# Gated linear attention and a gated MLP on one core: first batch in pairs of chunks

## The chip, the cores and the metric

The kernel runs on one core of a Trainium2 chip. A core has TensorE (PE in the profile; PEld is its loading of weights), VectorE (DVE), ScalarE (ACT), GpSimd (POOL) and SyncE (SP), and 16 DMA engines between the main memory and the on-chip memory of 128 partitions. TensorE writes to PSUM, which has eight banks of 128 partitions by 512 floats; DVE and ACT read it from there. The metric is the device time of one execution, in microseconds (us).

## The reference

Two layers, one after the other. The first is a recurrence over 768 tokens for 4 batches and 8 heads, with a 48 by 48 state:

```python
for t in range(S):
    state = alpha[:, :, t, :, None] * state + np.einsum('bhd,bhe->bhde', k[:, :, t], v[:, :, t])
    y[:, :, t] = np.einsum('bhd,bhde->bhe', q[:, :, t], state)
```

Its output, with the heads side by side, is x (4 x 768 x 384). The second layer mixes it:

```python
h = np.maximum(x @ w_in, 0.0)                      # 384 -> 1024
u, v = h[..., :512], h[..., 512:]
v_n = (v - mean(v)) / np.sqrt(var(v) + 1e-06)      # over the 512
v_s = np.einsum('ts,bsd->btd', w_spatial, v_n) + b_spatial[None, :, None]
out = (u * v_s) @ w_out                            # 512 -> 384
```

All arrays are float32 in main memory; the kernel multiplies in bf16.

## The kernel before

**First layer** (`first(i)`, i = 6 b + c). A batch is cut into six chunks of 128 tokens, one token per partition. For each chunk SP loads alpha, k, q and v (`ac`, `kc`, `qc`, `vc`, 192 KB each, rows of 48 floats; L231). ACT takes the logarithm of alpha (`la`, L268). A matmul with a triangle of ones gives its running sum over the tokens, and four one-column matmuls give its total per pair of heads (`cum`, L289 and L299). ACT makes `binv` = exp(−sum), `bc` = exp(total) and exp(sum); POOL multiplies k by `binv` (`kt`, L322), DVE multiplies q by exp(sum) (`qt`, L358), POOL casts v (`vb`, L366). TensorE transposes `kt` and `qt` in four 128x128 blocks each, in two PSUM banks (L375), and DVE or ACT copies each out (`kT`, `qT`). Scores are eight matmuls of 48 rows by 128 columns, two heads side by side in two row halves of the array (`pt`, L465); DVE multiplies them by a triangular mask (`ptm`, L477); `y` is eight matmuls of 48 columns with the masked scores (L494), and four of 96 columns with the state of the chunks before (L488). The state's growth is four matmuls of 96 columns over 128 output rows (`tp`, L421), of which the two diagonal halves are used: DVE adds them to the old state in two instructions on 64 partitions each (L438), POOL multiplies by `bc` (L447) and casts to `sbd` (L454, L455). y is cast, transposed in three blocks (L513) and copied to `xT`.

**Second layer**, per batch: `second_v` (v, relu, mean and variance, `vn`), `second_u`, `second_s` (the spatial mix: six matmuls of 384 columns per group, eight groups; bias added by DVE from `bsp_bc`, product with u on POOL, L664) and `second_o` (four matmuls per 128 tokens, a copy, a store on SP, L684). They share helper lines: L559 is every matmul of the second layer, L136 and L138 are copies on ACT and DVE. In the last batch the bias is put in by a matmul of one row (`ones_row` by `b_sp_sb`) at the head of each of the eight groups, and one DVE multiply ends a group (L648). `w_spatial` is transposed on TensorE once (`weights`, L570).

**Order.** Nothing is left to a scheduler at run time: each step is an `Op` with an engine, an estimated duration, dependencies, a priority and the PSUM slots that it takes. `schedule()` (L50) places the operations by estimated start and priority, and emits them in that order; every engine then runs its own list in order and waits by semaphores. PSUM has rings of two banks for `a` (cum, tp, y), two for `p` (transposes, scores) and four for `p2` (second layer). Loads and stores share SP's queue; w_in, w_spatial, w_out and the bias (a broadcast to 128 partitions, L702, and a row, L703) are loaded by POOL. Loads have four buffers (alpha, q) or six (k, v); stores have four. A path for two chunks at once is in the code, switched off by `FOLD = 0`.

## Time and profile before

| | |
|---|---|
| median of 3 runs | 169.93 us (169.17 to 170.67) |
| profiled execution | 169.51 us, of it 167.7 us span |
| busy: PE, PEld | 138.7 us, 87.1 us |
| busy: DVE, ACT, POOL | 123.0, 104.8, 85.5 us |
| DMA | 26.61 MB, mean 159 GB/s, 95% of the packets under 512 B |
| mean granted TensorE clock | 0.990 |

Times in the profile are microseconds from the span's start. "Busy" is the time in which an engine had an instruction under way; matmuls overlap, so a busy PE is not PE at its peak. A group is named by line, engine, operation, output and inputs, with the number of its instructions, their busy time, the mean of one in ns, and the idle time of the engine just before them with what ended it. In the slices, a digit is the busy share of a fortieth of the span in tenths.

### The profile page before, as it was taken

How to read it: one execution, taken by the hardware profiler on the slowest of the kernel's cores; microseconds unless marked ns; L12 is line 12 of the kernel's file. 1: busy time of each engine (PE TensorE's matmuls, PEld its weight loads, DVE VectorE, ACT ScalarE, POOL GpSimd, SP SyncE). 2: the span in 40 equal slices, each digit the busy share in tenths (PEclk: the TensorE clock that was granted, in tenths of full speed). 3: DMA queues.
4: the chain of work that ended last, by engine and by line, in shares of the span. 5: the costliest groups of instructions: out<-in, count | busy, mean ns of one | idle time of the engine just before them, and what ended most of it. 6: DMA issues, size and time to landing. Idle time of an engine off the chain costs nothing.

```text
span 167.7 us, 3952 instructions
## 1 busy us (share of the span) xinstructions
PE 138.7 (83%) x1402; PEld 87.1 (52%) x1412; DVE 123.0 (73%) x278; ACT 104.8 (62%) x255; POOL 85.5 (51%) x155
## 2 busy tenths in 40 slices
PE   0364687984579998999959999998999999999991
PEld 0252446553446765664526576664666665544450
DVE  7564568996648899879899787679999970883410
ACT  3432445984458846778869647998997546970042
POOL 7742508583152899953264898844369972000000
PEclk9999999999959999999999999999999999999999
DMA  5999989999699897396999891899992005200025
GB/s 115 217 181 209 223 164 215 170 201 253 133 197 219 167 218 145 86 287 154 215 217 210 172 216 51 209 266 181 199 227 56 0 4 207 76 0 4 0 101 182
DMA packets 105140, 26.61 MB, mean 159 GB/s; under 512 B 100320, under 2 KB 104672, under 8 KB 105120
## 3 DMA queue, kind: packets, MB, share of 16 engines
q1 hardware_dynamic: 103296, 23.60, 65.9%
q0 software_dynamic: 1824, 2.75, 9.1%
q8 instruction: 11, 0.18, 0.5%
q14 instruction: 9, 0.07, 0.1%
HBM read 23.99 MB, written 4.72 MB: 171 GB/s over the span
## 4 chain that ended last, share of the span: by engine, by line
PE 55%; DMA 13%; DVE 10%; ACT 9%; POOL 6%; issue 4%; DVEq 0%; POOLq 0%; ACTq 0%
PE ps L559 36%; DMA ac<-in_alpha_dram 6%; PE pt L375 5%; DMA w_in_sb<-in_moe_w_in_dram 5%; PE pt L465 3%; POOL kt L322 3%; PE y L513 3%; PE cum L289 2%; DMA qc<-in_q_dram 2%; PE tp L421 2%; DVE ptm L477 2%; ACT uT L142 2%; PE y L488 2%; DVE vn L612 2%; PE y L494 2%
## 5 line engine op out<-in xcount | busy, mean ns | idle before, releaser
L559 PE MATMUL ps<-w_spT,vn 128*128 128x384 bf16 x192 | 38.3, 326 | 0.0
L322 POOL TENSOR_TENSOR kt<-kc,binv 128x384 bf16<-128x384 f32 x24 | 21.9, 912 | 27.2 <-ACT bc L317 19.1
L477 DVE TENSOR_TENSOR ptm<-pt,mask 128x512 bf16<-128x512 f32 x48 | 31.1, 683 | 4.2 <-PE pt L465 3.9
L664 POOL TENSOR_TENSOR gT<-vsb,uT 128x384 bf16<-128x384 f32 x24 | 21.6, 912 | 2.3 <-DVE vsb L652 2.2
L559 PEld LDWEIGHTS <-vn 128*128 128x128 bf16 x192 | 16.4, 97 | 9.4 <-issue 1.4
L136 ACT COPY o_sb<-ps 128x384 f32<-128x384 f32 x22 | 10.5, 482 | 16.6 <-PE ps L559 16.1
L559 PE MATMUL ps<-w_in_sb,xT 128*128 128x512 bf16 x62 | 18.1, 407 | 2.7 <-DMA w_in_sb<-in_moe_w_in_dram 1.8
L594 DVE BATCH_NORM_STATS2 stats<-v_sb 128x6 f32<-128x512 bf16 x24 | 16.3, 678 | 5.3 <-ACT v_sb L142 5.3
L559 PE MATMUL ps<-xT,w_in_sb 128*128 128x384 bf16 x96 | 18.9, 328 | 0.7 <-ACT v_sb L142 0.7
L142 ACT ACTIVATE v_sb<-ps 128x512 bf16<-128x512 f32 x24 | 14.2, 595 | 6.0 <-PE ps L559 5.9
L559 PE MATMUL ps<-w_out_sb,gT 128*128 128x384 bf16 x96 | 17.7, 326 | 0.0
L310 ACT ACTIVATE binv<-cum 128x384 bf16<-128x384 f32 x24 | 11.8, 490 | 8.8 <-PE cum L299 6.6
L268 ACT ACTIVATE la<-ac 128x384 bf16<-128x384 f32 x24 | 12.5, 522 | 7.1 <-DMA ac<-in_alpha_dram 4.6
L366 POOL CAST vb<-vc 128x384 bf16<-128x384 f32 x24 | 12.1, 506 | 9.3 <-DMA vc<-in_v_dram 8.6
L358 DVE TENSOR_TENSOR qt<-qc,cum 128x384 bf16<-128x384 f32 x24 | 13.2, 550 | 4.5 <-DMA qc<-in_q_dram 2.1
L447 POOL TENSOR_TENSOR state<-state,bc 128x192 f32<-128x192 f32 x20 | 10.2, 512 | 11.2 <-DVE state L438 4.5
L652 DVE TENSOR_TENSOR vsb<-ps,bsp_bc 128x384 f32<-128x384 f32 x24 | 13.2, 554 | 2.9 <-PE ps L559 2.4
L289 PE MATMUL cum<-la,ut_ones 128*128 128x384 bf16 x24 | 8.8, 368 | 7.8 <-ACT la L268 7.8
L136 ACT CAST x_sb<-y 128x384 bf16<-128x384 f32 x24 | 11.5, 485 | 4.9 <-PE y L494 4.6
L375 PE MATMUL pt<-ident,kt 128*128 128x128 bf16 x96 | 10.2, 234 | 4.8 <-POOL kt L322 4.2
L142 ACT ACTIVATE uT<-ps 128x384 bf16<-128x384 f32 x30 | 13.6, 497 | 0.7 <-PE ps L559 0.7
L438 DVE TENSOR_TENSOR state<-tp,state 64x192 f32<-64x192 f32 x32 | 11.2, 350 | 3.7 <-PE tp L421 3.4
(75 smaller groups left out, 253.4 us busy)
## 6 DMA issues: line engine op xcount, KB each, us to landing
ac<-in_alpha_dram SPq DMA_DIRECT2D x24, 192.0 KB, 3.7
kc<-in_k_dram SPq DMA_DIRECT2D x24, 192.0 KB, 3.8
qc<-in_q_dram SPq DMA_DIRECT2D x24, 192.0 KB, 3.7
vc<-in_v_dram SPq DMA_DIRECT2D x24, 192.0 KB, 3.8
out_dram<-o_sb SPq DMA_DIRECT2D x24, 192.0 KB, 2.0
wsp_nat<-in_moe_w_spatial_dram POOLq DMA_DIRECT2D x1, 1152.0 KB, 13.1
w_in_sb<-in_moe_w_in_dram POOLq DMA_DIRECT2D x1, 768.0 KB, 8.6
w_out_sb<-in_moe_w_out_dram POOLq DMA_DIRECT2D x1, 384.0 KB, 7.7
```

The costliest lines, as they stand in the source:

```text
L136: nc.scalar.copy(out=out, in_=in_)
L142: nc.scalar.activation(out=out, in_=in_, func=AF.Relu)
L268: nc.scalar.activation(out=la[:, :, :, 0:D], in_=quad(st["ac"]), func=AF.Ln)
L289: nc.tensor.matmul(out=cm[:, 0:DM], lhsT=ut_ones, rhs=la[:, :, :, 0:D], start=True, stop=True)
L322: nc.gpsimd.tensor_mul(out=kt[:, :, :, 0:D], in0=quad(st["kc"]), in1=st["binv"])
L358: nc.vector.tensor_mul(out=qt[:, :, :, 0:D], in0=quad(st["qc"]), in1=st["cv"])
L375: nc.tensor.transpose(hold["t"][:, hp, :], src[:, hp, :, :], ident)
L477: nc.vector.tensor_tensor(out=st["ptm"][:, s], in0=st[f"pt{s}"], in1=mask4, op=ALU.mult)
L559: return lambda ps: nc.tensor.matmul(out=out(ps), lhsT=lhsT(), rhs=rhs(), start=start, stop=stop)
L594: nc.vector.bn_stats(out=stats, in_=d["v_sb"][:, tt, :])
L652: nc.vector.tensor_tensor(out=hold["vs"], in0=ps[:, 0:TH], in1=bsp_bc[:, th, :], op=ALU.add)
L664: nc.gpsimd.tensor_tensor(out=bt[b]["gT"][:, dsl, cols], in0=hold["vs"], in1=bt[b]["uT"][:, dsl, cols], op=ALU.mult)
```

## The change

Batch 0 is computed in three pairs of chunks (`pair(j)`). Each of its 12 loads (`load_pair`) brings 256 tokens, two neighbouring tokens to a partition, in rows of 96 floats. Chunk 0 of a pair then lies in partitions 0 to 63 and chunk 1 in 64 to 127, and each step is done for the even and the odd tokens (`par`): the running sums are two accumulating matmuls for each parity, the state's growth, the scores and the scores' part of y work on 64-row halves, and scores and growth also on 64-column halves of the array. The pair's sums and transposes use the `p2` banks.

In batches 1 to 3, q and k are transposed together into one bank and copied out by one instruction of 1024 columns, and the state's growth is eight matmuls of 48 columns on 64-column halves, so that DVE adds the state in one instruction on 128 partitions (in batch 0 as well).

`schedule()` now counts TensorE's activity in windows and doubles durations outside warm ones; where an operation that takes PSUM slots would leave TensorE idle before 24 us of its own reckoning, it puts matmuls of a constant tile (`junk`, up to 192 columns each) ahead of that operation, into the same bank. It also treats DMA as an engine with a duration for each transfer.

The bias is no longer broadcast by DMA: two one-row matmuls and two copies make `bsp_bc` (`bias()`); in the last batch only the last of the eight groups keeps its one-row matmul, and the others add and multiply as in the other batches, the product on POOL or DVE. Constants are set in three lots, two of them later; load buffers are six chunks for all four inputs, store buffers six. w_in is issued after the first logarithm, w_spatial and the bias after that of the third pair, w_out after its last q product.

The core of the diff (a line of "..." marks what is left out):

```diff
+class Clock:
+
+
+    TICK, ENOUGH = 3.4133, 3100.0
+
+    def __init__(self):
+        self.count = {}
+
+    def warm(self, t):
+        return self.count.get(int(t / self.TICK) - 1, 0.0) >= self.ENOUGH
+
+    def run(self, t, dur, cols):
+
+        end = t + dur * (1.0 if self.warm(t) else 2.0)
+        x = t
+        while x < end - 1e-9:
+            k = int(x / self.TICK + 1e-9)
+            y = min(end, (k + 1) * self.TICK)
+            self.count[k] = self.count.get(k, 0.0) + cols * (y - x) / (end - t)
+            x = y
+        return end
...
+        if eng == "PE":
+            if op.take and start < warm_to:
+                t = max([free.get(eng, 0.0), warm_from] + [slot.ring.free_at(k) for k, slot in enumerate(op.take)])
+                while True:
+                    each = 0.00042 if clock.warm(t) else 0.00084
+                    cols = min(192, int((start - t) / each) // 32 * 32)
+                    if cols < 96:
+                        break
+                    fill.append(cols)
+                    t = clock.run(t, 0.00042 * cols, cols)
+            end = clock.run(start, dur, op.cols)
...
+    def bank(pool, shape, dtype, **kw):
+
+        t = pool.tile(shape, dtype, **kw)
+        flat = t if len(shape) == 2 else t.rearrange("p a b -> p (a b)")
+        for cols in fill:
+            nc.tensor.matmul(out=flat[:, 0:cols], lhsT=junk[:, 0:128], rhs=junk[:, 0:cols], start=True, stop=True)
+        fill.clear()
+        return t
...
+        nc.vector.memset(junk, 0.5)
...
+    def dma(key, us, emit, deps, prio, eng="SP", issue=0.4):
+        o = op(key + ("issue",), eng, issue, emit, deps + [xfers[-8] if len(xfers) >= 8 and key[0] in LOADS else None],
+               prio=prio)
+        x = op(key, "DMA", us, lambda _: None, [o], prio=prio, lat=2.0)
+        if key[0] in LOADS:
+            xfers.append(x)
+        return x
...
+        def z(_):
+            st["state"] = work.tile([128, HP, D], FP32, name="state")
+            if c == 0:
+                nc.vector.tensor_copy(out=st["state"], in_=st["tp"])
+            else:
+                nc.vector.tensor_tensor(out=st["state"], in0=st["tp"], in1=T[i - 1]["state"], op=ALU.add)
+
+        op(("z", i), "DVE", 0.27, z, got(("upd", i), ("S", i - 1), ("sb", i - WK)), prio=P + 8, use=[st["sl_t"]])
...
+    def pair(j):
+
+        st = T[2 * j]
+        P = float(20 * j)
+        t0 = 2 * j * C
+        EV = {"DVE": 0.34, "ACT": 0.48}
+
+        def halves(ci):
+            return slice(64 * ci, 64 * ci + 64)
+
+        def ln(_):
+            nc.scalar.activation(
+                out=lap_bufs[j][:, :, :, 0:D], in_=st["ac"].rearrange("p h two d -> p two h d"), func=AF.Ln)
+
+        op(("lnp", j), "ACT", 0.73, ln, got(("acp", j), ("cz", j - 1)), prio=P + 1)
...
+            def cum(_, par=par, last=last):
+                cm = st[f"cum{par}"] = bank(pp_2, [128, 512], FP32, name="ps2")
+                for p2 in range(2):
+                    nc.tensor.matmul(
+                        out=cm[:, 0:DM], lhsT=lt_pair if p2 > par else le_pair, rhs=lap_bufs[j][:, p2, :, 0:D],
+                        start=(p2 == 0), stop=(p2 == 1))
+                if not last:
+                    rows = halves(par)
+                    for hp in range(HP):
+                        for p2 in range(2):
+                            nc.tensor.matmul(
+                                out=cm[:, DM + hp:DM + hp + 1],
+                                lhsT=lap_bufs[j][rows, p2, 2 * hp:2 * hp + 2, :].rearrange("p s d -> p (s d)"),
+                                rhs=ones_col[rows], start=(p2 == 0), stop=(p2 == 1))
+
+            op(("cump", j, par), "PE", 0.33 + 0.2, cum, got(("lnp", j)), prio=P + 2, take=sl_c[par], cols=768)
...
+            for nm, bufs in (("k", ktp_bufs), ("q", qtp_bufs)):
+                hold = {}
+                sl = Slot(rings["p2"])
+
+                def tr(_, par=par, bufs=bufs, hold=hold):
+                    pt = bank(pp_2, [128, 512], FP32, name="ps2")
+                    hold["t"] = pt.bitcast(BF16).rearrange("p (n t) -> p n t", n=8)[:, 0:HP, :]
+                    for hp in range(HP):
+                        nc.tensor.transpose(hold["t"][:, hp, :], bufs[j][:, par, hp, :, :], ident)
+
+                op(("tr", nm, j, par), "PE", 0.25, tr, got((nm + "tp", j, par)), prio=P + 5, take=sl, cols=512)
...
+                for hp in range(HP):
+                    for s in range(2):
+                        for par in range(2):
+                            nc.tensor.matmul(
+                                out=T[i]["tp"][64 * s:64 * s + 64, hp, :], lhsT=ktp_bufs[j][rows, par, hp, s, :],
+                                rhs=st["vb"][rows, par, 2 * hp + s, :], start=(par == 0), stop=(par == 1))
+
+            op(("upd", i), "PE", 0.43, upd,
...
+            def sc(_, par=par):
+                for s in range(2):
+                    st[f"pt{s}{par}"] = bank(pp_p, [128, HP, 128], FP32, name="pt")
+                for hp in range(HP):
+                    for s in range(2):
+                        for ci in range(2):
+                            rows = slice(64 * s, 64 * s + D)
+                            nc.tensor.matmul(
+                                out=st[f"pt{s}{par}"][halves(ci), hp, :], lhsT=st["kT"][rows, par, hp, halves(ci)],
+                                rhs=q_cols(rows, hp, ci), start=True, stop=True)
...
+                rows = halves(ci)
+                n, tot = 0, 2 * H + (HP if i else 0)
+                for h in range(H):
+                    for par in range(2):
+                        nc.tensor.matmul(
+                            out=yt[:, h, :], lhsT=st[f"ptm{par}"][rows, h % 2, h // 2, :],
+                            rhs=st["vb"][rows, par, h, :], start=(n == 0), stop=(n == tot - 1))
+                        n += 1
+                if i:
+                    for hp in range(HP):
+                        nc.tensor.matmul(
+                            out=yt[:, 2 * hp:2 * hp + 2, :].rearrange("p s d -> p (s d)"),
+                            lhsT=q_cols(slice(0, 128), hp, ci), rhs=sbd_bufs[(i - 1) % NB][:, hp, :],
+                            start=False, stop=(n == tot - 1))
...
+        def tr_qk(_):
+            pt = bank(pp_p, [128, 512], FP32, name="pt")
+            t = hold["t"] = pt.bitcast(BF16).rearrange("p (n t) -> p n t", n=8)
+            for n, src in enumerate((kt, qt)):
                 for hp in range(HP):
-                    nc.tensor.transpose(hold["t"][:, hp, :], src[:, hp, :, :], ident)
...
+                    nc.tensor.transpose(t[:, HP * n + hp, :], src[:, hp, :, :], ident)
+
+        def ev_qk(eng):
+            st["kqT"] = work.tile([128, 2, HP, C], BF16, name="kqT", bufs=4).rearrange("p a h c -> p (a h) c")
+            copy(eng, st["kqT"], hold["t"])
...
+        op(("trk", i), "PE", 0.46, tr_qk, got(("kt", i), ("qt", i), ("y", i - WK)), prio=P + 5, take=sl, cols=1024)
...
-                st["tp"] = pp_a.tile([128, HP, 2 * D], FP32, name="tp", tag="a")
+                st["tp"] = bank(pp_a, [128, HP, D], FP32, name="tp", tag="a")
                 for hp in range(HP):
-                    nc.tensor.matmul(
-                        out=st["tp"][:, hp, :], lhsT=kt[:, hp, :, :],
-                        rhs=st["vb"][:, 2 * hp:2 * hp + 2, :].rearrange("p s d -> p (s d)"),
-                        start=True, stop=True)
...
+                    for s in range(2):
+                        nc.tensor.matmul(
+                            out=st["tp"][64 * s:64 * s + 64, hp, :], lhsT=kt[:, hp, s, :],
+                            rhs=st["vb"][:, 2 * hp + s, :], start=True, stop=True)
+
+            st["sl_t"] = Slot(rings["a"])
+            op(("upd", i), "PE", 0.25, upd, got(("kt", i), ("vb", i), ("sb", i - WK), ("S", i - 1)), prio=P + 7, take=st["sl_t"], cols=384)
...
     def second_s(b, dsl, th):
-        tail = b == B - 1
+        last = b == B - 1 and dsl == NDS - 1 and th == 1
         mms = []
-        if tail:
+        if last:
             mms.append(mm(
                 lambda ps: ps[:, 0:TH], lambda: ones_row, lambda: b_sp_sb[:, th * TH:(th + 1) * TH], True, False))
         for st in range(NT):
...
+              us + got(("be", th)) + [made.get(("o", b - 2, x)) for x in range(NT)], parts=2, pdeps=pdeps)
+        if last:
             made[("g", b, dsl, th)] = made[("s", b, dsl, th)]
         else:
-            def gm(_):
-                nc.gpsimd.tensor_tensor(
+            def gm(eng):
+                ENG[eng].tensor_tensor(
                     out=bt[b]["gT"][:, dsl, cols], in0=hold["vs"], in1=bt[b]["uT"][:, dsl, cols], op=ALU.mult)
 
-            op(("g", b, dsl, th), "POOL", 0.82, gm, got(("s", b, dsl, th)), prio=Q)
+            op(("g", b, dsl, th), {"POOL": 0.82} if b < B - 1 else {"POOL": 0.82, "DVE": 0.46}, None, gm, got(("s", b, dsl, th)), prio=Q)
 
...
     def b_sp(_):
-        nc.gpsimd.dma_start(out=bsp_bc, in_=moe_b_spatial[None, :].to_broadcast([128, S]))
         nc.gpsimd.dma_start(out=b_sp_sb, in_=moe_b_spatial[None, :])
 
...
+    def load_pair(j):
+        st = T[2 * j]
+        t0 = 2 * j * C
+        for n, (name, src) in enumerate((("ac", alpha), ("kc", k), ("qc", q), ("vc", v))):
+            def emit(_, name=name, src=src):
+                t = io_pool.tile([128, 2, H, D], FP32, name=name)
+                t = st[name] = t.rearrange("p a h d -> p (a h d)").rearrange("p (h two d) -> p h two d", two=2, d=D)
+                nc.sync.dma_start(
+                    out=t.rearrange("p h two d -> p h (two d)"),
+                    in_=src[0, :, t0:t0 + 2 * C, :].rearrange("h (p two) d -> p h (two d)", two=2))
+
+            dma((name + "p", j), 1.52, emit, [], LOADPRIO[j][n])
...
+        if j == 0:
+            dma(("w_in",), 2.2, w_in, got(WIN), 0.0, "POOL", 1.0).lat = 8.0
+            op(("consts2",), "POOL", 2.5, constants2, got(("sb", 1)), prio=60.0)
+        if j == 2:
+            dma(("w_sp",), 3.3, w_sp, got(WSP), 0.0, "POOL", 1.0).lat = 8.0
+            dma(("b_sp",), 0.1, b_sp, got(WSP), 0.0, "POOL", 1.0)
+            dma(("w_out",), 1.1, w_out, got(WOUT), 0.0, "POOL", 1.0).lat = 8.0
...
-    schedule(ops)
+    schedule(ops, fill, 2.0, WARM)
```

496 lines of the change are left out of this document (265 added, 231 removed).

## The prediction

> **What bounds the kernel now.** I read the page first: the span in slices, then the DMA queues.
>
> ```profile
> PE   0364687984579998999959999998999999999991
> PEclk9999999999959999999999999999999999999999
> DMA  5999989999699897396999891899992005200025
> q1 hardware_dynamic: 103296, 23.60, 65.9%
> q0 software_dynamic: 1824, 2.75, 9.1%
> ```
>
> PE is half idle in the first eleven slices (46 us) while DMA stands at 9; after that PE stands mostly at 9. So there are two stages, and I cut the trace there with the view by stretches of time (columns: length, then busy time and instructions of PE, PEld, DVE, ACT, POOL, then granted clock, DMA share, GB/s).
>
> ```profile
> 0.00:46.20 46.20, 26.57 (x301) 19.10 (x305) 32.55 (x80) 23.39 (x55) 23.11 (x52) 1.00 1.00 189
> 46.20:164.00 117.80, 112.13 (x1101) 68.03 (x1107) 90.41 (x198) 80.92 (x200) 62.39 (x104) 0.99 0.67 147
> 40.00:50.00 10.00, 6.20 (x81) 4.59 (x83) 5.05 (x11) 4.62 (x9) 3.33 (x6) 0.83 0.90 188
> 80.00:90.00 10.00, 7.40 (x69) 4.63 (x71) 9.22 (x21) 7.92 (x24) 3.38 (x7) 1.00 1.09 215
> 164.00:167.70 3.70, 0.00 (x0) 0.00 (x0) 0.00 (x0) 0.48 (x1) 0.00 (x0) 1.00 0.45 163
> ```
>
> Up to 46.2 us the DMA share is 1.00, and PE is busy 26.57 us of 46.2: loads bound this stage. From 46.2 to 164 PE is busy 112.13 of 117.8 us and DMA has room (0.67): PE, with what feeds it, bounds that one. Then the last store lands. The chain of waits (start, length, what) says the same:
>
> ```profile
> 4.51 0.53 ACT la L268
> 7.11 8.62 DMA w_in_sb<-in_moe_w_in_dram
> 36.70 9.45 DMA ac<-in_alpha_dram
> 76.92 3.75 DMA qc<-in_q_dram
> 141.82 22.19 PE ps L559 x120
> 164.08 0.48 ACT o_sb L136
> ```
>
> The first work starts at 4.51, the chain hangs 8.62 us on w_in and 9.45 us on an alpha load that is queued behind the weights, once more on a q load at 77, and ends in matmuls. The execution took 169.51 us for a span of 167.7 (1.8 outside), 0.4 under the median of 169.93; I sum on 169.51 and add 0.4.
>
> **The change part by part.**
>
> *Fewer, longer packets for batch 0: −6.3 us of DMA.*
>
> ```profile
> ac<-in_alpha_dram SPq DMA_DIRECT2D x24, 192.0 KB, 3.7
> out_dram<-o_sb SPq DMA_DIRECT2D x24, 192.0 KB, 2.0
> bsp_bc<-in_moe_b_spatial_dram POOLq DMA_DIRECT2D x1, 384.0 KB, 7.9
> ```
>
> A chunk load is 1024 packets of 192 B (128 tokens by 8 heads by 48 floats); a store is 128 packets of 1536 B. After 164 us only stores move: 163 GB/s x 3.7 us = 603 KB, three stores, in 0.45 x 3.7 = 1.67 us of all 16 engines, so 0.55 us each, 69 ns per packet on one engine (8 packets each). Queue q1 took 0.659 x 167.7 = 110.5 us; less 24 x 0.55 = 13.3 leaves 97.2 us for 96 loads: 1.01 us each, 15.8 ns per packet. A line through the two points gives 0.0396 ns per byte, so 23.4 ns for the new 384 B packet and 64 x 23.4 = 1.50 us for a pair load, against 2.02 for the two loads it replaces. Twelve pair loads save 12 x 0.52 = 6.3 us. No row has a packet of 384 B: if a packet costs by the byte, the saving is 0; if by the count alone, 12.1. I take the line, since its ends are both measured. The Trainium skill, "DMA: Bandwidth & Descriptors" (Specifications), says that transfers under 512 B are done as a read-modify-write; both 192 and 384 lie under it. The measured rise from 11 to 22 B per ns between 192 and 1536 B does not tell where it happens, so the time by that rule is a rival below.
>
> *Bias no longer broadcast by DMA: −2.2 us of DMA.* q0 took 0.091 x 167.7 = 15.3 us for 2.75 MB; bsp_bc is 0.39 MB of it: 2.2 us (1.2 if what is read counts, where the weights are twice as large). It lies in the queue ahead of the alpha load at 36.70. Two matmuls and two copies replace it, in PE's idle part of the first stage.
>
> Together 8.5 us at a share of 1.00: the first stage can end at about 37.7 instead of 46.2. The other moves on the queues: SP issues the same bytes in 12 fewer instructions; w_in on POOL's queue goes out after the first Ln instead of after the first kt, some 1.5 us earlier; w_sp, w_out and the bias row stay behind the last third of batch 0, as before.
>
> *Batch 0 costs PE more.* Prices from start to start in a dense part of the order of time:
>
> ```profile
> 121.80 0.33 PE L289 MATMUL cum<-la,ut_ones 128*128 128x384 bf16 x1
> 121.96 0.24 PE L299 MATMUL cum<-ones_col,la 128*128 128x1 bf16 x4
> 122.07 0.65 PE L559 MATMUL ps<-xT,w_in_sb 128*128 128x384 bf16 x3
> ...
> 127.96 0.33 PE L421 MATMUL tp<-vb,kt 128*128 128x96 bf16 x4
> 128.13 0.65 PE L559 MATMUL ps<-w_spT,vn 128*128 128x384 bf16 x3
> 128.72 0.40 PE L465 MATMUL pt<-qT,kT 48*128 48x128 bf16 x8
> 129.05 0.34 PE L513 MATMUL y<-ident,x_sb 128*128 128x128 bf16 x3
> ...
> 137.68 0.36 PE L494 MATMUL y<-vb,ptm 128*128 128x48 bf16 x8
> 137.88 0.81 PE L559 MATMUL ps<-w_out_sb,gT 128*128 128x384 bf16 x4
> ```
>
> A 384-column matmul takes 0.16 us, four one-column ones 0.11, four of 96 columns 0.17, eight score matmuls 0.33, eight of 48 columns 0.20. Per pair: two more 384-column and eight more one-column matmuls for the sums of logarithms, 0.32 + 0.22 = 0.54; 32 instead of 16 scores, +0.66; state update 32 of 48 columns for 8 of 96, 0.80 − 0.34 = +0.46; 16 more matmuls of 48 columns in y, +0.40. That is 2.1 us, 6.2 for three pairs. Four tiles of 64x64 may run beside each other, so the scores may add nothing: 4.2.
>
> Changing the shape of the array costs on top. Its price stands in the tail, where a one-row bias matmul opens each group:
>
> ```profile
> 149.27 0.33 PE L559 MATMUL ps<-b_sp_sb,ones_row 1*128 1x384 bf16 x1
> 149.53 0.66 PE L559 MATMUL ps<-w_spT,vn 128*128 128x384 bf16 x3
> 150.13 0.33 PE L559 MATMUL ps<-b_sp_sb,ones_row 1*128 1x384 bf16 x1
> ```
>
> From 149.27 to 150.13 are 0.86 us for the bias and three full matmuls; three take 0.48, so the bias costs 0.37, of which 0.16 is its own and 0.21 the way into and out of another shape. A pair makes about eight such round trips (sums, updates, scores, y, twice each) where two chunks made two: +1.3, +3.8 for three. So batch 0 adds 4 to 10 us of PE. PE's cover in the first stage is 46.2 − 26.6 = 19.6 us idle, 11 once the stage is 8.5 shorter, but the 4.5 before the first Ln, and waits inside the first pair, can't be filled. I charge 3 us, between 0 and 10. The longer chain of a pair is a rival.
>
> *Junk matmuls and the clock: −0.8 us.*
>
> ```profile
> 26.41 0.52 PE L494 MATMUL y<-vb,ptm 128*128 128x48 bf16 x8
> 30.76 0.36 PE L494 MATMUL y<-vb,ptm 128*128 128x48 bf16 x8
> 42.42 0.36 PE L494 MATMUL y<-vb,ptm 128*128 128x48 bf16 x8
> ```
>
> The same eight matmuls take 0.52 us at 26.4 and 0.36 at 30.8 and later: PE starts slow though the clock row shows 9, and after the wait at 44 to 46 the clock row falls to 5 (0.83 over 40 to 50 us, 1.7 us of work lost). While loads bound the stage, a faster PE shortens only the steps between a landing and the next, so the early warmth pays little. If the wait for alpha goes, the 1.7 goes; I count half. A junk matmul of 192 columns stands in PE's queue ahead of real work where the planner's times are late: by the row of 384 columns, at half speed, under 0.2 us each, at most one per wait. Between −1.7 and +1.
>
> *64-column state update in batches 1 to 3: +2.3 us.* 15 chunks go from four matmuls of 96 columns (0.17) to eight of 48 (0.20 by the y row, 0.10 if two run side by side), and enter and leave a new shape: 0.21. Bounds 15 x (−0.07) = −1.0 and 15 x 0.24 = 3.6; I take 0.15 a chunk, as some sit next to the scores, which change shape anyway. The Trainium skill, "TensorEngine Tiling (Array Packing)" (Key Properties), says that a change of tiling mode drains TensorE; the bias rows agree, with 0.21 us. By that rule every one of the 15 pays, and the sum would be 1.3 higher.
>
> *Bias in the tail: −2.6 us.* Seven of the eight one-row matmuls go, at 0.37. They lie on the last 22.19 us of the chain. In their place DVE adds and POOL or DVE multiplies; eight groups of some 1 us each leave room for one 0.55 add each, and the last group keeps its matmul, so what is late is no later.
>
> *DVE and SP in the second stage: −1.8 us.*
>
> ```profile
> L438 DVE TENSOR_TENSOR state<-tp,state 64x192 f32<-64x192 f32 x32 | 11.2, 350 | 3.7 <-PE tp L421 3.4
> L477 DVE TENSOR_TENSOR ptm<-pt,mask 128x512 bf16<-128x512 f32 x48 | 31.1, 683 | 4.2 <-PE pt L465 3.9
> L138 DVE COPY qT<-pt 128x512 bf16<-128x512 bf16 x14 | 5.9, 418 | 1.5 <-PE pt L375 1.3
> ```
>
> One state add instead of two saves DVE 0.35 us a chunk, the merged copy some 0.1. PE is the bound there, so I count 0.5 us in all (0 to −3). The merged transposes wait for both q and k; the matmuls of the earlier batch that fill PE stand ahead of or behind them, and the price is inside these bounds. PE idles 2.6 us between 80 and 90, after the q load at 76.92 that left SP's queue late; ac and qc buffers grow from four to six chunks and stores from four to six, so I count half, −1.3 (0 to −2.6).
>
> **Sum.** −8.5 + 3.0 − 0.8 + 2.3 − 2.6 − 0.5 − 1.3 = −8.4: 161.1, and 161.5 against the median.
>
> **Rivals.**
>
> *A. The forecast:* 161.5; its own range by the terms 157 to 166. Chance 0.60.
>
> *B. A packet costs by the byte up to a store's size.* The 6.3 us stay, but then the slower first stage hides all that batch 0 adds (3.0): 161.1 + 6.3 − 3.0 + 0.4 = 164.8; with the wait for alpha left, 165.6. For it: nothing between 192 and 1536 B is measured. Against: the line. The Trainium skill's rule on transfers under 512 B ("DMA: Bandwidth & Descriptors", Specifications) would do this here. Chance 0.13.
>
> *C. The pair's chain becomes the bound, slower.* Chunk 0 took from 4.51 to its last copy:
>
> ```profile
> 13.19 0.48 ACT L136 COPY xT<-y 128x384 bf16<-128x384 bf16 x1 [0.73 <-PE y L513]
> ```
>
> ```profile
> L358 DVE TENSOR_TENSOR qt<-qc,cum 128x384 bf16<-128x384 f32 x24 | 13.2, 550 | 4.5 <-DMA qc<-in_q_dram 2.1 <-ACT cum L353 2.0
> ```
>
> 9.2 us. A pair repeats the DVE steps (one 0.55, two copies of 0.42, two masks of 0.68, 0.70 of state: 3.4) and four ACT steps of 0.5 (as the la and xT rows): 14.6 us. If the three pairs run one after another, y of the last ends at 4.5 + 3 x 14.6 = 48.3 instead of 42.8: +5.5, no gain from DMA, the second stage's terms −2.1: 169.9 + 3.4 = 173.3. The gain is gone from 12.8 us a pair, and over 14.0 the kernel is slower by 1%. Against: y of chunks 2 and 3 stand 4.35 us apart (26.41, 30.76), so chunks do overlap. Chance 0.08.
>
> *D. The second stage also had slack:* PE's busy time counts overlapping matmuls (0.33 us for one that gives way after 0.16). If the lighter DVE and PSUM use let PE close up, and batch 0 hides all its extra: 161.5 − 3.0 − 2.5 (DVE to its bound) − 1.0 = 155. Chance 0.15.
>
> *E. The gain is eaten inside TensorE:* batch 0 shows all its 10 us and every update its bound, 161.5 + 7 + 1.3 = 169.8. Chance 0.04.
>
> **How the numbers follow.** About 1% is what a measurement here can tell from no change. Faster by over 1% (under 168.2): A, B, D nearly whole, 0.86. Slower (over 171.6): C, less the part where the chain is only a little too long, 0.07. Same: 0.07. The range 155 to 168.5 takes A, B and D's upper half, and leaves out C, E and D's far end.
>
> **What would show it.** Right: DMA at 9 from the start with the first stage ending near 38; pair loads near 1.5 us of engine time; no 8.6 us on w_in; the last 120 matmuls some 2.6 us shorter; tp groups with a gap of 0.1 on either side. Wrong: pair loads at 2 us (B); PE or DVE at 9 already in batch 0, with y of chunk 5 after 42 us (C); PE's second stage shorter than its 117.8 us by far more than 4 (D).

## The result and the profile after

Before took 169.55 us in these runs (median of 4, 167.97 to 170.67), after 163.16 us (4 runs, 162.83 to 163.89): a ratio of 0.966, with a 95% interval of 0.958 to 0.974. The profiled execution of after took 163.89 us, 162.1 of it span. Some executions of a kernel come out over 1.5% longer than its fastest: medians are of all executions, ratios leave these out.

The page of after, the span in 40 slices and the DMA queues:

```profile
PE   7599798089999999989999999999999999999991
PEclk9959999557999999999999999999999999999999
DMA  5999999999979898897999998989700002600025
q1 hardware_dynamic: 90816, 23.60, 66.4%
q0 software_dynamic: 1744, 2.36, 8.2%
```

PE is fuller than before in the first eleven slices, but there is a 0 in the eighth slice (28.4 to 32.4 us), and from that slice on the clock row reads 5, 5, 7. The view by stretches, with the same columns as in the prediction, cut where chunk 7's sum of logarithms begins and where the last copy begins:

```profile
0.00:47.35 47.35, 37.30 (x563) 27.13 (x564) 32.30 (x76) 25.34 (x58) 20.07 (x45) 0.86 1.04 208
47.35:158.55 111.20, 109.12 (x1156) 68.84 (x1155) 89.34 (x187) 75.01 (x185) 65.37 (x106) 1.00 0.64 142
27.80:33.20 5.40, 0.01 (x1) 0.01 (x1) 0.01 (x1) 0.95 (x3) 0.64 (x1) 0.56 1.21 206
30.00:40.00 10.00, 6.80 (x70) 4.59 (x71) 4.56 (x11) 4.62 (x10) 0.10 (x1) 0.57 1.09 195
40.00:50.00 10.00, 9.84 (x149) 6.68 (x147) 7.97 (x18) 8.80 (x22) 4.91 (x10) 1.00 0.92 181
80.00:90.00 10.00, 9.63 (x97) 5.86 (x96) 9.83 (x25) 9.53 (x27) 5.46 (x11) 1.00 0.97 198
```

Three marks split both spans. Chunk 7's sum of logarithms (the first `cum` row in each fence) is the first; the first matmul of the tail's spatial mix (149.27 before, 146.28 after) the second; the start of the last copy the third (164.08 before, 158.55 after). In order of time, first before, then after:

```profile
46.75 0.48 PE L289 MATMUL cum<-la,ut_ones 128*128 128x384 bf16 x1 [2.69 <-ACT la L268]
...
54.63 0.33 PE L289 MATMUL cum<-la,ut_ones 128*128 128x384 bf16 x1
```

```profile
47.35 0.32 PE L581 MATMUL cum<-lap,ut_ones 128*128 128x384 bf16 x1
...
52.77 0.33 PE L581 MATMUL cum<-lap,ut_ones 128*128 128x384 bf16 x1
...
146.28 6.99 PE L735 MATMUL ps<-w_spT,vn 128*128 128x384 bf16 x42
153.20 0.33 PE L735 MATMUL ps<-b_sp_sb,ones_row 1*128 1x384 bf16 x1
```

| | before, us | after, us | change | forecast |
|---|---|---|---|---|
| start to chunk 7's sum | 46.75 | 47.35 | +0.6 | −6.3 (−8.5 + 3.0 − 0.8) |
| to the tail's spatial mix | 102.52 | 98.93 | −3.6 | +0.5 (+2.3 − 0.5 − 1.3) |
| to the start of the last copy | 14.81 | 12.27 | −2.5 | −2.6 |
| to the end of the span | 3.62 | 3.55 | −0.1 | 0 |

The total came near the forecast of 161.5, and two of its three parts did not. The first stage, where nearly the whole gain was to come from, gained nothing. The chain of waits of after says what holds it (start, length, what):

```profile
19.62 12.61 DMA vc<-in_v_dram
32.25 0.51 ACT vbp L180
...
158.55 0.48 ACT o_sb L180
```

The wait of 8.62 us for w_in and that of 9.45 us for an alpha load are gone, but one of 12.61 us for v of the third pair stands in their place. The order of time around it, on four engines:

```profile
7.37 1.44 SPq L905 DMA_DIRECT2D qc<-in_q_dram  x1
...
20.29 0.89 POOL L890 DMA_DIRECT2D wsp_nat<-in_moe_w_spatial_dram  x1
...
21.46 0.83 ACT L371 ACTIVATE lap<-ac 128x768 bf16<-128x768 f32 x1
...
32.25 0.51 ACT L180 CAST vbp<-vc 128x384 bf16<-128x384 f32 x1 [6.70 <-DMA vc<-in_v_dram]
...
33.20 0.50 PE L342 MATMUL y<-ident,x_sb 128*128 128x128 bf16 x3 [5.52 <-ACT x_sb L180]
```

SP issues v at 19.62, POOL issues w_spatial (1152 KB) 0.7 us later, and v lands 12.6 us after its issue. Meanwhile ACT stands 6.70 us at the cast of v; copies of y of chunks 2 and 3 (`x_sb`) are queued behind it, so PE, which has nothing else, waits 5.52 us for `x_sb`. From 27.8 to 33.2 PE is busy for 0.01 us. In before w_spatial went out at 27.79:

```profile
27.79 0.90 POOL L696 DMA_DIRECT2D wsp_nat<-in_moe_w_spatial_dram  x1
```

### The profile page after: what moved, and what is told of

It is laid out like the page before. It is cut to its first block, busy times and chain, and to the rows that moved or that the text cites. A ratio compares the mean times of both kernels' runs of the same rounds, so it can differ in the third digit from the quotient of the medians.

```text
span 162.1 us, 4501 instructions
## 1 busy us (share of the span) xinstructions
PE 146.4 (90%) x1718; PEld 96.0 (59%) x1718; DVE 121.6 (75%) x263; ACT 100.8 (62%) x243; POOL 85.4 (53%) x151
## 4 chain that ended last, share of the span: by engine, by line
PE 55%; SPq 11%; DVE 10%; DMA 8%; ACT 8%; POOL 4%; issue 3%; ACTq 0%; DVEq 0%; POOLq 0%
PE ps L735 37%; SPq L905 11%; DMA vc<-in_v_dram 8%; PE pt L633 4%; PE y L342 2%; DVE ptm L674 2%; POOL gT L856 2%; DVE stats L786 2%; PE pt L663 2%; ACT cum L611 2%; PE tp L649 2%; DVE qtp L616 2%; PE cum L581 2%; PE ps L746 1%; ACT x_sb L180 1%
## 5 line engine op out<-in xcount | busy, mean ns | idle before, releaser
L856 POOL TENSOR_TENSOR gT<-vsb,uT 128x384 bf16<-128x384 f32 x28 | 25.5, 922 | 19.9 <-DVE vsb L844 19.7
L674 DVE TENSOR_TENSOR ptm<-pt,mask 128x512 bf16<-128x512 f32 x36 | 23.3, 683 | 2.9 <-PE pt L663 2.7
L735 PE MATMUL ps<-w_in_sb,xT 128*128 128x512 bf16 x72 | 19.6, 396 | 0.2 <-ACT xT L180 0.2
L844 DVE TENSOR_TENSOR vsb<-ps,bsp_bc 128x384 f32<-128x384 f32 x31 | 16.5, 554 | 3.0 <-PE ps L735 2.5
L605 POOL TENSOR_TENSOR ktp<-kc,binv 128x384 bf16<-128x384 f32 x18 | 16.5, 917 | 3.0 <-POOL sbd L321 1.3
L342 PE MATMUL y<-ident,x_sb 128*128 128x128 bf16 x72 | 8.4, 228 | 6.5 <-ACT x_sb L180 6.5
L735 PEld LDWEIGHTS <-gT 128*128 128x128 bf16 x96 | 8.9, 98 | 5.5
L735 PEld LDWEIGHTS <-w_in_sb 128*128 128x128 bf16 x96 | 8.5, 97 | 5.8 <-issue 0.2
L342 PEld LDWEIGHTS <-x_sb 128*128 128x128 bf16 x72 | 5.2, 100 | 9.9 <-ACT x_sb L180 7.8
L182 DVE COPY xT<-y 128x384 bf16<-128x384 bf16 x10 | 4.2, 416 | 8.8 <-PE y L342 8.7
L616 DVE TENSOR_TENSOR qtp<-qc,cum 128x384 bf16<-128x384 f32 x18 | 9.8, 547 | 0.8 <-ACT cum L611 0.8
```

The costliest lines, as they stand in the source:

```text
L342: nc.tensor.transpose(xv[:, ks, :], st["x_sb"][:, ks, :], ident)
L605: nc.gpsimd.tensor_mul(out=kt[:, :, :, 0:D], in0=quad(st["kc"]), in1=st["binv"])
L616: nc.vector.tensor_mul(out=qt[:, :, :, 0:D], in0=quad(st["qc"]), in1=st["cv"])
L674: nc.vector.tensor_tensor(out=st["ptm"][:, s], in0=st[f"pt{s}"], in1=mask4, op=ALU.mult)
L735: return lambda ps: nc.tensor.matmul(out=out(ps), lhsT=lhsT(), rhs=rhs(), start=start, stop=stop)
L844: nc.vector.tensor_tensor(out=hold["vs"], in0=ps[:, 0:TH], in1=bsp_bc[:, th, :], op=ALU.add)
```

## The experiments

The theories were: (1) the early w_spatial load takes the bandwidth from v and with it the first stage's gain; (2) the 64-column update, the junk matmuls or the longer chain of a pair cost what is missing; and for the middle, whether it gained from the update, from the buffers, or from what the first stage hands on. Each ratio is to executions of before made beside that run on the same chip; their medians lie between 167.44 and 168.24 us.

### w_spatial later

The loads of w_spatial and of the bias row are issued right before that of w_out; the written order of everything else stays.

```diff
@@ w_sp, b_sp (issue after the third pair's logarithm)
-        nc.gpsimd.dma_start(out=..., in_=...)
+        pass
@@ w_out
+        w_sp_late()
+        b_sp_late()
```

> The changed kernel with one move: the loads of w_spatial and of the bias row are issued right before that of w_out (about 27 us) instead of at 20 us; the order of everything else is kept. Theory 1 (the weights' long packets hold back v of the third pair, which landed 12.6 us after its issue, and all engines stand from 27.8 to 33.2): v lands within 6 us of its issue, the stand of 5.4 us goes, PE's clock stays up, and the kernel takes 158 to 160 instead of 163.2; what may be late next is w_spatial itself at its transposes, up to 2 us. Theory 2 (batch 0 is bound by TensorE or by the pair's chain, not by that load): 162.2 to 163.5.

Measured: 159.6 us (159.32 to 163.31, 4 runs), ratio 0.959 (0.946 to 0.972). The profiled execution has a span of 157.6. Its DMA issues (KB each, median us to landing), after's row first and then this kernel's:

```profile
vc<-in_v_dram SPq DMA_DIRECT2D x3, 384.0 KB, 10.9
```

```profile
vc<-in_v_dram SPq DMA_DIRECT2D x3, 384.0 KB, 6.6
```

In order of time, this kernel casts v at 26.00 and has chunk 7's sum at 42.83, 4.5 us before after's 47.35; the span is 4.5 us shorter.

```profile
26.00 0.51 ACT L180 CAST vbp<-vc 128x384 bf16<-128x384 f32 x1 [0.65 <-DMA vc<-in_v_dram]
...
35.52 0.34 PE L531 MATMUL y<-sbd,kqT 128*128 128x96 bf16 x4
...
37.60 3.81 PE L746 MATMUL ps<-ident,wsp_nat 128*128 128x128 bf16 x36 [1.57 <-DMA wsp_nat<-in_moe_w_spatial_dram]
...
42.83 0.32 PE L581 MATMUL cum<-lap,ut_ones 128*128 128x384 bf16 x1
```

Theory 1 holds for the first stage. What is late next is w_spatial itself, by 1.57 us at its transposes. The gain up to there is larger than the 4.5 us: the last matmuls of y of chunk 5 start at 35.52 here and at 43.28 in after, 7.8 us apart. Some 3 us of it are lost again in that wait and in the 36 transposes behind it, which take 3.81 us here (106 ns each, at a granted clock of 0.55) and 2.30 in after (64 ns each, at 1.00):

```profile
43.63 2.30 PE L746 MATMUL ps<-ident,wsp_nat 128*128 128x128 bf16 x36
```

### Without the junk matmuls

All 69 junk matmuls are left out, once from after and once from the version above; they compute nothing that is used.

```diff
-        for cols in fill:
-            nc.tensor.matmul(out=flat[:, 0:cols], lhsT=junk[:, 0:128], rhs=junk[:, 0:cols], ...)
```

> The changed kernel with its 69 junk matmuls left out and the order otherwise kept. Prediction's term (early warmth pays 0.8 us at most, as loads bound the stage): 163 to 164.2. Theory 2 (TensorE is what batch 0 waits for, and junk stands ahead of real work): 161 to 162.5. A rival for junk: without it PE stays at half speed through the first pairs, and each step of the chain is later: 164.5 to 166.

> The kernel of e1 without the 69 junk matmuls, order kept. Theory (the pairs' chain waits for loads, DVE and ACT, not for TensorE's speed): 159 to 160.5, as without junk the changed kernel did not move. Rival (in the changed kernel the stand at 28 to 33 us made the clock fall in either case and hid what junk is worth; here it shows): 161 to 162.5.

Measured: 163.38 us (162.92 to 163.69) against after's 163.16; with w_spatial later 158.66 us (157.88 to 159.93; ratio 0.946, 0.938 to 0.953) against 159.6. The junk is worth nothing in either. The first matmul of the kernel takes 0.48 us without it, and with it 0.32 in after but again 0.48 in the version with w_spatial later. What is faster with it is the second pair: its first sum takes 0.33 instead of 0.50 us. In order of time, both with w_spatial later, without junk and then with it:

```profile
13.79 0.50 PE L380 MATMUL ps<-lap,le_pair 128*128 128x384 bf16 x1
```

```profile
14.93 0.33 PE L382 MATMUL ps<-lap,le_pair 128*128 128x384 bf16 x1
```

That sum starts later with junk, which stands in PE's list right ahead of it. By y of chunk 5 the version with junk is 1.5 us ahead (35.52 against 37.02), but both then wait for w_spatial, whose transposes start at 37.60 and 38.10: the first stage waits for loads, and a faster step between two landings ends at the same landing. Without junk the transposes run at a granted clock of 1.00 (2.18 us), and chunk 7's sum comes at 41.70, 5.1 us before that of the kernel before. This version has the lowest median of the study; it beats both kernels.

### 192-byte packets again

The version with w_spatial later, each pair load split into its even and its odd tokens: the same bytes to the same places, in packets of 192 B.

```diff
-    nc.sync.dma_start(out=t, in_=src[...])
+    for n2 in range(2):
+        nc.sync.dma_start(out=t[:, :, n2, :], in_=src[...].rearrange(
+            "h (p two) d -> p h two d", two=2)[:, :, n2, :])
```

> The kernel of e1 (w_spatial issued later, 159.6 us) with each of the 12 pair loads made as two loads of 192-byte packets into the same places (even tokens, odd tokens); order kept. Prediction's line of 15.8 ns for 192 B and 23.4 ns for 384 B: two short loads take 2.0 us instead of 1.5, so 6.3 us more of DMA by the end of batch 0, v of the third pair lands about 6 us later, and 4 to 6 us of it show: 163.5 to 166. Cost by the byte: no difference, 159 to 160.5.

Measured: 167.31 us (165.38 to 169.09, 10 runs), 7.7 more than with whole rows. The stretch of 10 to 20 us, with whole rows and then with split ones:

```profile
10.00:20.00 10.00, 8.52 (x173) 6.44 (x172) 6.59 (x16) 5.09 (x14) 4.71 (x11) 1.00 1.17 251
```

```profile
10.00:20.00 10.00, 6.60 (x95) 5.34 (x93) 3.68 (x8) 1.84 (x3) 2.67 (x7) 0.67 1.01 193
```

The rate falls from 251 to 193 GB/s. In the chain of waits the long wait comes back, at 33.83 for an alpha load:

```profile
33.83 12.74 DMA ac<-in_alpha_dram
```

Not all of the 7.7 us need be the packets. The last matmuls of y of chunk 5 start at 40.46, 4.9 us after the 35.52 with whole rows; after them the chain hangs on that alpha load, which here goes out 1.5 us behind w_spatial (32.38), a second wait of the kind that the first experiment took away. The edit also makes 24 loads of 12 and keeps the order written for whole rows, and neither is told apart from the size of the packets. At 4.9 to 7.7 us the longer packets are still the largest single gain in the change, once the load that takes their place is out of the way. The rule of the Trainium skill, "DMA: Bandwidth & Descriptors" (Specifications), that transfers under 512 B are a read-modify-write, doesn't separate these two kernels, as 192 and 384 B both lie under it; the runs do.

### The cast of v on POOL

In after, the two casts of v of the third pair move from ACT to POOL, so that the copies of y are no longer queued behind them.

```diff
 def emit(eng):
+    eng = "POOL" if j == 2 else eng
```

> The changed kernel (w_spatial early) with the two casts of v of the third pair issued to POOL, which is idle from 28 us, instead of ACT; everything else in the same order. Theory (what stands from 27.8 to 33.2 is ACT's queue: the cast that waits for v stands ahead of the copies of y of chunks 2 and 3, which need nothing from it): x of chunks 2 and 3 comes at 27.5 though v still lands at 32, TensorE works on, 160 to 162. Rival (the load's lateness itself sets the stage's end, since the third pair's y needs v): 162.7 to 163.5.

Measured: 163.36 us (162.59 to 164.1), no gain. The stand is gone; from 27.6 to 33.0 PE is busy for 3.42 us instead of 0.01:

```profile
27.60:33.00 5.40, 3.42 (x55) 2.48 (x51) 3.94 (x10) 2.52 (x5) 0.93 (x2) 1.00 1.12 205
```

But v comes no earlier, and chunk 7's sum moves by 0.9 us (order of time):

```profile
32.07 0.50 POOL L182 CAST vbp<-vc 128x384 bf16<-128x384 f32 x1 [5.12 <-DMA vc<-in_v_dram]
...
46.48 0.32 PE L582 MATMUL cum<-lap,ut_ones 128*128 128x384 bf16 x1
```

So it is the lateness of the load that sets the end of the stage, and what waits in ACT's queue behind it only shows it.

### The tail's bias alone

Before, with only the change of the bias in the tail: seven groups without the one-row matmul, add on DVE, product on POOL or DVE.

```diff
-        tail = b == B - 1
+        tail = b == B - 1 and dsl == NDS - 1 and th == 1
@@
-            op(("g", b, dsl, th), "POOL", 0.82, gm, ...)
+            op(("g", ...), {"POOL": 0.82} if b < B - 1 else {"POOL": 0.82, "DVE": 0.46}, None, gm, ...)
```

> The kernel before with only the last batch's bias changed: seven of eight one-row matmuls go, DVE adds the bias from the broadcast tile and POOL or DVE multiplies. Prediction's term: -2.6 us, 166.5 to 167.5 against 169.6. Rival (the sum and product now come after one another and the last output matmuls wait for them): 168.5 to 170.

Measured: 165.35 us (161.67 to 166.07, 4 runs) against 168.24, −2.9, a difference without an interval. The trace settles the tail itself: from the first matmul of its spatial mix, at 147.08, to the start of the last copy, at 159.39, are 12.31 us, where before had 14.81 and after has 12.27.

```profile
147.08 6.99 PE L559 MATMUL ps<-w_spT,vn 128*128 128x384 bf16 x42
```

In after's rows above, too, the 42 matmuls of the tail's spatial mix run in one piece of 6.99 us, and one one-row matmul is left, at 153.20.

### The 64-column update, four ways

After with the update of batches 1 to 3 as it was (four matmuls of 96 columns, two adds on 64 partitions), the rest of the order kept:

```diff
-    st["tp"] = bank(pp_a, [128, HP, D], ...)
+    st["tp"] = bank(pp_a, [128, HP, 2 * D], ...)
@@ upd: for hp in range(HP)
-    for s in range(2): matmul(out=tp[64*s:64*s+64, hp, :], lhsT=kt[:, hp, s, :], rhs=vb[:, 2*hp+s, :])
+    matmul(out=tp[:, hp, :], lhsT=kt[:, hp, :, :], rhs=vb[:, 2*hp:2*hp+2, :])
@@ z: one add of 128 partitions
+    becomes two adds of 64 partitions for i >= NCH
```

> The changed kernel with the state update of batches 1 to 3 as before: four matmuls of 96 columns on the whole array and two adds on 64 partitions each; order kept. Prediction's terms: TensorE gives 2.3 us back and the lighter DVE loses 0.5, so 161 to 162. Rival (in the second stage DVE is what TensorE waits for at 80 to 90 us, and one add less was the gain): 163.5 to 165.5.

Measured: 167.9 us (167.19 to 169.71, 10 runs), 4.7 slower than after, beyond both expectations. That looked like a large worth of the new update, until before was given it: in its written order, and then with the planner told of one add and the new duration.

```diff
@@ before
-    op(("upd", i), "PE", 0.2, upd, ...)     four matmuls of 96 columns
+    op(("upd", i), "PE", 0.25, upd, ...)    eight of 48, 64-column halves
-    for s in range(2): op(("z", i, s), "DVE", 0.27, z(s), ...)
+    op(("z", i), "DVE", 0.27, z, ...)
```

> The kernel before with only the state update changed: eight matmuls of 48 columns on 64-column halves and one add of 128 partitions in place of two, in all batches; order kept. Prediction's terms, TensorE +2.3 and DVE -0.5: 1 to 2 us slower than before. Theory after e3 (DVE is what the second stage waits for, 0.35 us for each of 20 chunks): 3 to 6 us faster than before.

> The kernel before with the state update of e8 (eight matmuls on 64-column halves, one add), and the planner told so: one add of 0.27 us in place of two, 0.25 us of TensorE for 0.2. e3 lost 4.7 us where the order was planned for one add and two were run; e8 won nothing where the order was planned for two and one was run. If the written order decides what a shorter DVE step is worth, this is 2 to 5 us faster than before. If the update is worth nothing by itself and e3 lost for another reason (a shift of its loads and stores), it is within 1 us of before.

Measured: 168.79 us (166.02 to 171.28, 10 runs) in the order of before, against 168.21: ratio 0.998 (0.991 to 1.005). Replanned: 169.51 us (168.56 to 169.73) against 167.44: ratio 1.014 (1.004 to 1.024), slower by 2.1 us, outside both expectations. The last of the four is the first again, now with the planner told of the two adds:

```diff
@@ the kernel with the old update in after, planner told
+    op(("z0", i), "DVE", 0.27, ...); op(("z", i), "DVE", 0.27, ...)
-    op(("upd", i), "PE", 0.25, ...)
+    op(("upd", i), "PE", 0.2, ...)
```

> The changed kernel with the state update of batches 1 to 3 as before (as e3: four matmuls of 96 columns, two adds), and the planner told so: two adds of 0.27 us, 0.2 us of TensorE for 0.25. e3 lost 4.7 us with the order planned for one add; on the kernel before the same update was worth nothing with the old order (e8) and lost 2 with its own (e9). If e3's loss is that two adds were run in an order written for one: 161.5 to 164.5, the update is worth about nothing here too. If the shorter DVE step is what the second stage of the changed kernel lives on: 166.5 to 168.5.

Measured: 162.74 us (162.41 to 163.08), 0.4 under after. So the new update gains nothing in either kernel, and most of the 4.7 us measured the order: two adds run in places written for one. The stretch of 120 to 130 us in after, then with the old update in after's order, then with the old update replanned:

```profile
120.00:130.00 10.00, 10.00 (x102) 6.24 (x100) 9.27 (x21) 6.59 (x19) 4.39 (x7) 1.00 0.01 2
```

```profile
120.00:130.00 10.00, 8.24 (x75) 4.89 (x73) 9.80 (x22) 8.04 (x23) 4.77 (x9) 1.00 0.01 2
```

```profile
120.00:130.00 10.00, 10.00 (x125) 6.94 (x124) 9.41 (x19) 4.38 (x9) 7.98 (x14) 1.00 0.01 2
```

In after's order DVE is then at 9.80 of 10 us and PE falls to 8.24, with no load under way (DMA share 0.01); replanned, PE is full again.

### The buffers alone

Before with six buffers for alpha and q, and for stores.

```diff
-    IO3 = 4
+    IO3 = 6
-    outp = ...(name="outp", bufs=4)
+    outp = ...(name="outp", bufs=6)
```

> The kernel before with six buffers instead of four for alpha and q, and six for the stores, as the changed kernel has them. Prediction's term for the q load that came late at 77 us: -1.3, between 0 and -2.6. Rival (the late q load is a matter of SP's order around the stores, not of buffers): within 0.5 of before.

Measured: 166.44 us (164.49 to 168.74, 10 runs) against 167.44: ratio 0.997 (0.991 to 1.002), which doesn't tell it from none. Its stretch of 80 to 90 us:

```profile
80.00:90.00 10.00, 8.66 (x97) 5.53 (x96) 8.85 (x22) 8.46 (x23) 6.82 (x12) 1.00 0.98 193
```

PE is busy for 8.66 us, where before had 7.40 and after has 9.63. That isn't shown to be the buffers' doing, as the same stretch fills without them too: in before with only the tail's bias changed, and in before with the new update replanned, both with four buffers and the old loads (the same columns, in this order):

```profile
80.00:90.00 10.00, 8.77 (x90) 5.62 (x90) 9.75 (x24) 8.88 (x25) 4.68 (x9) 1.00 1.02 197
```

```profile
80.00:90.00 10.00, 9.62 (x104) 5.77 (x106) 9.79 (x25) 9.36 (x26) 4.69 (x9) 1.00 0.98 193
```

### w_spatial later, replanned

The fastest version again, but the planner is told that w_spatial goes out behind the third pair's last q product, and that the two weight loads take twice as long. No junk here either.

```diff
-    WIN, WSP, WOUT = ("lnp", 0), ("lnp", 2), ("qtp", 2, 1)
+    WIN, WSP, WOUT = ("lnp", 0), ("qtp", 2, 1), ("qtp", 2, 1)
-    dma(("w_sp",), 3.3, ...)     dma(("w_out",), 1.1, ...)
+    dma(("w_sp",), 6.6, ...)     dma(("w_out",), 2.2, ...)
```

> The changed kernel without junk, with w_spatial issued after the third pair's last q product, as in e1 and e6, and the planner told so and given 6.6 and 2.2 us instead of 3.3 and 1.1 for the loads of w_spatial and w_out, so that it puts the transposes of w_spatial later. e1 waited 1.6 us there and its clock fell to 0.89 between 30 and 40 us. If that wait is what is left of the first stage: 156.5 to 158. If the waits inside the pairs are: as e6, 158 to 159.5.

Measured: 164.71 us (163.76 to 166.34), 6 us more than the same loads in the order written for the earlier w_spatial. The expectation missed. The stretch of 40 to 50 us:

```profile
40.00:50.00 10.00, 6.38 (x77) 4.49 (x76) 5.59 (x13) 3.58 (x7) 3.23 (x7) 0.70 1.02 199
```

POOL issues w_spatial at 27.05 here, at 27.41 in the first experiment, so the load is the same in time. But ACT stands at the logarithms of chunks 8 and 9, whose alpha loads haven't landed, with a copy of y queued behind (order of time):

```profile
43.13 0.52 ACT L573 ACTIVATE lap<-ac 128x384 bf16<-128x384 f32 x1 [2.78 <-DMA ac<-in_alpha_dram]
...
46.79 0.52 ACT L573 ACTIVATE lap<-ac 128x384 bf16<-128x384 f32 x1 [2.68 <-DMA ac<-in_alpha_dram]
47.22 0.46 ACT L178 CAST x_sb<-y 128x384 bf16<-128x384 f32 x1
```

The loads themselves are no later than in the fastest version: the second of them goes out at 42.94 here and at 43.66 there. What moved is ACT's list. There the same logarithm stands behind other work and waits for nothing; here the new order puts it ahead of work that was ready, and PE waits 2.10 us for the copy of y behind it. From the fastest version, in order of time:

```profile
43.66 0.74 SPq L552 DMA_DIRECT2D ac<-in_alpha_dram  x1
...
47.21 0.51 ACT L573 ACTIVATE lap<-ac 128x384 bf16<-128x384 f32 x1
```

## Why the prediction was right and wrong

The time was right, 163.16 against 161.5, 1.7 us off, in the middle of the range; the way to it was right in part, and that the total is near is in part luck: the first stage came out 6.9 us worse than forecast and the middle 4.1 better.

**The step that failed** is the sentence "w_sp, w_out and the bias row stay behind the last third of batch 0, as before". In the plan that is so; in time it isn't. Before, w_spatial followed a cast of v on POOL itself, so it couldn't go out ahead of that. Now it stands behind the third pair's logarithm, which is ACT's, and nothing in the load waits for it: POOL came to it at 20.29, ACT to the logarithm at 21.46. I priced w_in's move on POOL's queue and gave w_spatial's no price. It cost the gain that the first stage had: with the load put back (the first experiment) chunk 7's sum stands at 42.83, 3.9 us before the kernel before, instead of 47.35, 0.6 after it, and the kernel is 3.6 us faster than after. Of the forecast 6.3, 2.4 stay missing even then. The trace shows them at w_spatial's transposes: up to y of chunk 5 the gain on after is 7.8 us, and a wait of 1.57 and transposes slower by 1.5 take some 3 of it back.

**Packets: right in effect.** SP's queue, when full, issues a pair load every 1.48 us in after (4.41, 5.89, 7.37 in its order of time, of which the row at 7.37 is shown), where I had 1.50; with w_in under way the next ones take 2.8 to 3.6. Split packets cost 7.7 us against 6.3 forecast, 4.9 of them up to y of chunk 5. Rival B (cost by the byte), which had no difference there, is out. The measure under the term was weaker than I took it for: I read a DMA share of 1.00 as full. With whole rows the share reads 1.17 at 251 GB/s, with split ones 1.01 at 193, so the times of packets overlap. The packet time of queue q1 fell only from 110.5 us (in the prediction) to 0.664 x 162.1 = 107.6, a saving of 2.9 and not 6.3, while in the stretch shown the bytes per us are 30% more with whole rows.

**Rival C** named its sign, "y of chunk 5 after 42 us": it came at 43.3. Its mechanism was not there: with the same chain of a pair, but w_spatial later, y of chunk 5 came at 35.5 and the stage ended 4.5 us earlier. A sign that two causes share doesn't tell them apart.

**Batch 0's 3.0 us of PE:** not measured by itself. PE was busy for 37.30 us of the first 47.35, against 26.57 of 46.2 before (junk included), and still waited for loads.

**Junk and clock, −0.8:** nothing by the two runs without junk. The clock loss that I hoped to halve moved: 0.83 at 40 to 50 before became 1.00, and 0.57 stands at 30 to 40, after the stand of 5.4 us. The Trainium skill, "TensorE: Matmul & The Clock Gate" (Why this matters), says that an idle gap of some 3 us takes TensorE back to half its clock; the trace agrees for the stand of 5.4 us, with the digits 5 5 7 from the 0 of the PE row on. The length of a gap alone doesn't decide it here: in the version with w_spatial later a wait of 1.57 us was enough for 106 ns a transpose, while in before, in order of time, the transposes behind a wait of 2.38 us took 63 ns each:

```profile
40.90 1.51 PE L570 MATMUL ps<-ident,wsp_nat 128*128 128x128 bf16 x24 [2.38 <-DMA wsp_nat<-in_moe_w_spatial_dram]
```

Keeping it warm is worth what waits for it, here nothing.

**The 64-column update, +2.3, with DVE's −0.5:** +2.1 in before when replanned, +0.4 in after. The price per chunk was about right. In order of time, after:

```profile
120.58 0.39 PE L633 MATMUL pt<-ident,qtp 128*128 128x128 bf16 x4
120.90 0.31 PE L649 MATMUL tp<-vb,ktp 128*64 128x48 bf16 x8
121.14 0.66 PE L735 MATMUL ps<-xT,w_in_sb 128*128 128x384 bf16 x3
```

From the start of the transposes to that of the next group are 0.56 us, of which four transposes of 128 columns take about 0.22 (512 columns at the prediction's 0.16 for 384): 0.34 for the update, where I had 0.17 for the old one and up to 0.41 for the new. In after the stretch around it is full on DVE too (9.27 of 10). That the add which it saves pays for it fits the equal totals with either update, but isn't shown by itself.

**The tail, −2.6:** −2.5 in the trace of after, and −2.5 in that of before with the tail's change alone. Right.

**The middle, +0.5 forecast, −3.6 measured:** the terms were too small, and the −1.3 for buffers and SP is not shown to be theirs. From chunk 7's sum to chunk 8's were 7.88 us before and are 5.42 now, −2.5: no cold clock there any more. Between 80 and 90 us PE gained 9.63 − 7.40 = 2.2, where I had counted half of 2.6. These make 4.7, and 1.1 of it is lost elsewhere in the middle, where the dearer update stands. Two SP rows at about the same time show how far the loads are ahead, before and then after:

```profile
46.11 0.63 SPq L231 DMA_DIRECT2D ac<-in_alpha_dram  x1
```

```profile
47.44 1.13 SPq L554 DMA_DIRECT2D ac<-in_alpha_dram  x1
```

The first is the alpha load of chunk 8, the second that of chunk 10. So the bytes that shorter packet time freed in the first stage did go somewhere: into loads two chunks ahead, eight loads or some 8 us of queue at the 1.01 us a load of the prediction, while the one load that everything waited for stood beside w_spatial. That the packets make this lead is shown by the two versions with w_spatial later: with whole rows the alpha load at 46.65 is chunk 10's, with split ones that at 46.56 is chunk 8's. Whether that lead, the six buffers or the new order takes the stall at 80 to 90 away stays open: the buffers alone gave 1.0 us on before, which the interval doesn't tell from zero, and in before with the new update replanned the stall is gone (9.62 of 10 us) with neither lead nor buffers.

## What to carry to other kernels

A large load on another queue has its own issue time, and moving its trigger moves it: ask which small load on the critical path will then be under way beside it, and price that. DMA time that is saved pays only if the load that is awaited gets it. And where the order is written out ahead, an edit that changes a duration has to be measured with its order replanned, and a replanned order with the old one beside it: the same update was worth +4.7 or −0.4 us, and the same loads 158.7 or 164.7, by the order alone.

## What the runs showed of the hardware

A 384 KB load issued 0.7 us ahead of a 1152 KB load on another queue took 12.6 us instead of about 6.6, while the core moved 209 GB/s (19.6 to 32.2 us). The mean packet is 1.35 KB in q0, the weights' queue, and 0.26 KB in q1, by the page's packets and MB; that their size is the cause isn't shown, as no run changes the weights' packets. The Trainium skill, "DMA: Bandwidth & Descriptors" (Queues, rings and completion order), says that a DMA engine serves its queues in turn, a packet at a time; the trace agrees in direction, if turns go by packets as the page of the profile counts them, since the queue with the longer ones then gains. The other surprise was that a DMA share of 1.00 is not full: 1.17 was reached at 251 GB/s.
